# The eleventh first product on 64 rows between score matmuls, in ten maxima steps of a gated attention and mixture-of-experts kernel

## The chip, the core and the metric

One core of one Trainium2 chip runs the kernel. The metric is the device time of one execution in microseconds (us). Before the change it is 1328.08 us, the median of 3 runs (1327.91 to 1328.63).

## The reference

```python
def _A_ref(x, wqkv, wo):                       # S = 2048, D = 448, H = 16, Dh = 28
    q, k, v = qkv.reshape(B, S, 3, H, Dh)...   # qkv = x @ wqkv
    p = _softmax(einsum("bhqd,bhkd->bhqk", q, k) * Dh ** -0.5)
    return (p @ v).reshape(B, S, D) @ wo
def _B_ref(x, w_gate, w1, w2):                 # E = 8 experts, F = 1792, the best 2 of each token
    topk_idx = argsort(-(xf @ w_gate))[:, :2]
    for e in range(E):
        w = (softmax(topk_val) * (topk_idx == e)).sum(-1, keepdims=True)
        out = out + w * (_silu(xf @ w1[e]) @ w2[e])
def reference(...):
    g = _sigmoid((x * gate_w).sum(-1, keepdims=True))
    return g * _A_ref(x, ...) + (1 - g) * _B_ref(x, ...)
```

## The kernel before

The program runs in three stages: projections and routing (to about 118 us), the eight experts (118 to about 822 us), and the attention (to the end). Each number is carried as a high part and a low part, and a product of two of them is done as high times high, high times low and low times high.

An expert `e` works on its tokens in two halves `hf` of seven blocks `f` of 128 hidden columns. In a first product, 448 input features are contracted: three blocks of 128 rows, three matmuls each, and a fourth block of 64 features whose 128 rows hold the high part (rows 0 to 63) and the low part (rows 64 to 127) of the tokens. So a block has `NM` = 11 matmuls, and the eleventh is the low weights by that fourth block. The tokens go in `NC` pieces of `HC` columns: two pieces of 288, 276 and 264 columns in experts 0 to 2, one piece of 512 in experts 3 to 5, one of 504 and 480 in the last two. ScalarE then takes SiLU of the sum. The second products take seven hidden blocks by three matmuls of 448 columns for each of four blocks of 128 tokens; in experts 0 to 2 `last_slots` does the few tokens behind the 512th in 14 or 28 small matmuls into 64 or 32 columns of the array.

The softmax needs the maximum of every row of scores, and these maxima are found between the experts' matmuls. `max_stream` gives out 1024 *cells*. A cell is a matmul of one head's 28 rows (a query block of 128 by 512 keys) into one bank of PSUM. Head `j` of a group of four sits at rows `32j`, so that four cells run side by side. VectorE (DVE) reduces each bank to one column of `mp`. A *step* gives out six cells into the two tiles `pm1` and `pm0` of three banks each, or seven, with the accumulator that is not in use as the first bank (`spare`). The first four cells of a step go to four different heads, the other two or three follow as a second round. A six-bank step's fourth cell writes the second `pm` tile, and so waits until VectorE has read that tile's banks of the step before.

Where steps stand is written by hand in `STEPS`: for each expert and half a list of places among the first products (11 for each piece) and one among the second products. A place says after how many matmuls a step comes; a positive number is a seven-bank step, a negative one a six-bank step. `behind` looks the places up, and `step` runs the generator once. The engines' streams are in the order in which the code is written. `last_slots` is issued after as many second products as the first entry of the second list says. In the second halves, VectorE also transposes blocks of the next expert's tokens (`turn_blocks`, L230). In the trace, L134 are the cells, L148 and L155 their reductions, L1030 the first products, L1088 the second products, L945 `last_slots`, L292 and L684 matmuls of the first stage.

Of the kernel before, what the change touches and what calls it, by code (L numbers as in the profile page):

```python
# [2 lines left out]

# [47 lines left out]
SCALE = float(DH) ** -0.5  # L51
KR = DH + 1
# [12 lines left out]
def tile_gated_mha_moe(ctx: ExitStack, tc: tile.TileContext, x, xe_, xT, wv, wqk, wo, w1, w2, out):  # L65
# [53 lines left out]

    def max_stream():  # L120
        cells = [(g, qt, kc, j) for g in range(NG) for qt in range(NT) for kc in range(4) for j in range(4)]
# [3 lines left out]
        b = 0  # L125
        yield
        while b < len(cells):
            more = len(spare)
            step = cells[b:b + 6 + more]
            pm = [pmx.tile([128, 3, 512], F32, name=f"pm{h}") for h in range(2)][::-1]  # L130
            banks = spare[:] + [pm[n // 3][:, n % 3] for n in range(len(step) - more)]
# [4 lines left out]
            for g, qt, kc, j in step:  # L136
                if kc == 0 and j == 0 and qt % 4 == 0:
# [3 lines left out]
                if g + 1 < NG and j == 3:  # L141
# [4 lines left out]
            o = b % 256  # L146
            if more:
                nc.vector.tensor_reduce(mp[:, o:o + 1], banks[0], axis=AX.X, op=ALU.max)  # L148
            o += more

            n_m = len(step) - more
            cuts = sorted({0, min(3, n_m), min(n_m, max(0, 256 - o)), n_m})
            for lo, hi in zip(cuts, cuts[1:]):
                h = lo // 3
                nc.vector.tensor_reduce(mp[:, (o + lo) % 256:(o + lo) % 256 + hi - lo], pm[h][:, lo - 3 * h:hi - 3 * h],  # L155
# [1307 lines left out]
```

## Time and profile before

| | |
|---|---|
| median of 3 runs | 1328.08 us |
| profiled execution | 1328.14 us |
| its span | 1326.3 us |
| TensorE (PE) busy, share of span | 1321.1 us, 100% |
| weight loads (PEld) busy | 928.2 us, 70% |
| VectorE (DVE) busy | 1068.2 us, 81% |
| ScalarE (ACT) busy | 838.3 us, 63% |
| GpSimd (POOL) busy | 858.1 us, 65% |

The span is the time from the first to the last instruction of one profiled execution. Ends of matmuls are modelled, so neighbouring matmuls overlap in the rows; what one matmul takes of the engine is read from one start to the next. "Idle before" a weight load means only that no other load ran just before it.

### The profile page before, as it was taken

The numbers are of one execution on the slowest core, as the hardware profiler recorded it, in microseconds if no ns is written. First come the engines' busy times: TensorE is split into PE (matmuls) and PEld (weight loads), VectorE is DVE, ScalarE is ACT, GpSimd is POOL, SyncE is SP. The second block draws the span as 40 slices with busy tenths as digits, with TensorE's granted clock in tenths as the row PEclk, the third lists the DMA queues.
The fourth block names the chain that finished last, engine by engine and source line by source line (L and its number), as shares of the span: only waits on it lengthen the run. The fifth ranks groups of instructions, "written<-read, shape, count | busy, mean of one in ns | idle before, by whom it ended". The sixth has DMA issues, their size and how long they took to land. (4 is left out here: it accounts for less than half of the span.)

```text
span 1326.3 us, 32115 instructions
## 1 busy us (share of the span) xinstructions
PE 1321.1 (100%) x12210; PEld 928.2 (70%) x12210; DVE 1068.2 (81%) x1686; ACT 838.3 (63%) x1268; POOL 858.1 (65%) x1144
## 2 busy tenths in 40 slices
PE   9999999999999999999999999999999999999999
PEld 8888888788887777777777777555555555555558
DVE  5746898888898888989889886777788887777785
ACT  6316354365354344543444434999999999999981
POOL 2044877777687788786887854666666666666641
PEclk9999999999999999999999999999999999999999
DMA  9888757554553474545745423212422532342214
GB/s 352 291 259 270 212 160 185 154 159 107 169 149 89 148 207 146 165 100 156 187 120 171 106 78 71 56 41 70 115 54 72 118 75 49 75 111 52 51 41 137
DMA packets 138134, 176.65 MB, mean 133 GB/s; under 512 B 24255, under 2 KB 105857, under 8 KB 137465
## 3 DMA queue, kind: packets, MB, share of 16 engines
q1 hardware_dynamic: 119273, 145.58, 36.9%
q0 software_dynamic: 18560, 28.77, 10.5%
q8 instruction: 96, 1.57, 0.5%
q14 instruction: 61, 0.50, 0.1%
q10 hardware_dynamic: 144, 0.23, 0.1%
HBM read 124.51 MB, written 53.18 MB: 134 GB/s over the span
## 5 line engine op out<-in xcount | busy, mean ns | idle before, releaser
L155 DVE TENSOR_REDUCE mp<-pm 128x3 f32<-128x1536 f32 (+1 forms) x300 | 508.3, 1736 | 13.1 <-PE pm L134 12.5
L1319 PE MATMUL z<-P,V 128*32 128x288 f32 x4064 | 246.7, 383 | 0.4 <-ACT P L1276 0.2
L796 PE MATMUL z<-Q,K 29*128 29x512 f32 x762 | 225.7, 424 | 0.0
L796 PE MATMUL s<-Q,K 29*128 29x512 f32 x2286 | 224.9, 424 | 0.0
L1319 PEld LDWEIGHTS z<-P,V 128*32 128x32 f32 x4064 | 107.6, 109 | 132.5 <-ACT P L1276 47.1
L1104 ACT ACTIVATE yo<-acc,cg 128x448 f32<-128x448 f32 x64 | 40.6, 635 | 232.2 <-PE acc L1088 211.1
L867 POOL TENSOR_TENSOR w2l<-w2r,w2h 128x448 fp32r<-128x448 f32 x112 | 130.1, 1162 | 87.6 <-ACT w2h L861 64.7
L1285 ACT ACTIVATE P<-s 128x1536 f32<-128x1536 f32 x127 | 185.6, 1461 | 0.0
L1277 ACT ACTIVATE P<-s 128x1536 f32<-128x1536 f32 x127 | 183.6, 1446 | 0.0
L1088 PE MATMUL acc<-w2h,hh 128*128 128x448 f32 (+2 forms) x448 | 166.9, 373 | 0.3 <-PEq L881 0.3
L1088 PE MATMUL acc<-w2h,hl 128*128 128x448 f32 (+2 forms) x448 | 166.6, 372 | 0.0
L1088 PE MATMUL acc<-w2l,hh 128*128 128x448 f32 (+2 forms) x448 | 165.8, 370 | 0.0
L1035 ACT ACTIVATE hf<-acc 128x512 f32<-128x512 f32 (+8 forms) x154 | 73.7, 478 | 134.7 <-PE acc L1030 125.2
L796 PEld LDWEIGHTS z<-Q,K 29*128 29x128 f32 x762 | 121.7, 184 | 49.7 <-DVE osb L1331 39.4
L148 DVE TENSOR_REDUCE mp<-acc 128x1 f32<-128x512 f32 x131 | 90.2, 689 | 78.4 <-PE pm L134 69.3
L796 PEld LDWEIGHTS s<-Q,K 29*128 29x128 f32 x2286 | 125.6, 184 | 38.7 <-ACT P L1285 32.8
L876 POOL TENSOR_TENSOR hl<-hf,hh 128x512 fp32r<-128x512 f32 (+2 forms) x112 | 144.4, 1289 | 1.1 <-ACT hh L1038 1.1
L1030 PE MATMUL acc<-xeh,w1h 128*128 128x512 f32 (+5 forms) x408 | 136.2, 338 | 0.0
L1030 PE MATMUL acc<-xeh,w1l 128*128 128x512 f32 (+5 forms) x408 | 135.8, 338 | 0.0
L1331 DVE TENSOR_TENSOR osb<-z,osb 128x288 f32<-128x288 f32 x224 | 95.1, 425 | 40.3 <-PE z L1319 30.0
L1278 DVE TENSOR_SCALAR X<-z 128x512 f32<-128x512 f32 x127 | 87.9, 692 | 42.4 <-PE z L796 33.2
L1292 POOL TENSOR_SCALAR pu<-X 128x160 f32<-128x160 f32 x126 | 42.0, 333 | 122.4 <-DVE X L1278 120.9
(239 smaller groups left out, 2824.4 us busy)
## 6 DMA issues: line engine op xcount, KB each, us to landing
w2r<-in_w_dram SPq DMA_DIRECT2D x112, 224.0 KB
w1r<-in_w_dram SPq DMA_DIRECT2D x56, 384.0 KB
x_d<-xf SPq DMA_DIRECT2D x115, 64.0 KB
ys_d<-zero_d SPq DMA_DIRECT2D x32, 224.0 KB
qk_d<-hi SPq DMA_DIRECT2D x28, 256.0 KB
qk_d<-lo SPq DMA_DIRECT2D x28, 256.0 KB
w1r<-in_w_dram SPq DMA_DIRECT2D x112, 64.0 KB
Q<-qk_d SPq DMA_DIRECT2D x64, 112.0 KB
```

What stands on the lines that cost most here:

```text
L148: nc.vector.tensor_reduce(mp[:, o:o + 1], banks[0], axis=AX.X, op=ALU.max)
L155: nc.vector.tensor_reduce(mp[:, (o + lo) % 256:(o + lo) % 256 + hi - lo], pm[h][:, lo - 3 * h:hi - 3 * h], axis=AX.X, op=ALU.max)
L796: nc.tensor.matmul(banks[j], k[rw, kt % 8 // 4, ks], q[rw, c], start=i == 0, stop=i == 2)
L867: nc.gpsimd.tensor_tensor(w2l, w2r, w2h.bitcast(F32), op=ALU.subtract)
L876: nc.gpsimd.tensor_tensor(hl, hf32, hh.bitcast(F32), op=ALU.subtract)
L1030: mm = nc.tensor.matmul(pu[:, 0:HC], a, b[:, cs], start=i == 0, stop=i == len(mms) - 1)
L1088: mm = nc.tensor.matmul(py[:n, 0:D], a[:, cs], b, start=i == 0, stop=i == 3 * NH - 1)
L1277: nc.scalar.activation(P[:, 1:4], t[0], AF.Exp, scale=SCALE)
L1278: nc.vector.tensor_scalar(X, z[1], LAM * SCALE * math.log2(math.e), -126.0 * LAM, op0=ALU.mult, op1=ALU.max)
L1285: nc.scalar.activation(P[:, 4:7], t[1], AF.Exp, scale=SCALE)
L1319: mm = nc.tensor.matmul(po[32 * j:32 * j + 32, cs], v[:, kt % 8, 32 * j:32 * j + 32], P[4 * i + j][:, cs], start=i == 0, stop=i == 1)
L1331: nc.vector.tensor_tensor(accs[u][:, cs], po[:, cs], accs[u][:, cs], op=ALU.add)
```

## The change

Ten six-bank steps are moved to places that are multiples of 11: place 154 in both halves of experts 0 and 1, in both halves of expert 2, place 22 in the second half of expert 2, and place 11 in the second halves of experts 3 to 5. There the eleventh first product is not issued by itself. It is handed to the step as a function, takes rows 0 to 63 of its two operands alone, and is issued between the first four cells and the other two. So the low weights by the low tokens of the fourth block are left out in these ten products.

Cells are now counted for each head apart (`at`). In a step with a product, heads 2 and 3 (rows 64 to 127) give two cells and heads 0 and 1 one. In the other steps the heads that are behind give two. `lay_out` tries the orders of the cells and takes the one with the fewest reductions, since a reduction takes several banks only where the cells' columns are neighbours. Loads of queries and keys are issued once every head has passed the cell that called for them. `last_slots` comes after four second products everywhere.

```diff
 STEPS = [
-    (([17, 41, 71, 96, 127], [-1, -4, 18, 35, 52, 70]), ([-5, 28, 61, 94, 127], [-1, -4, 18, 35, 53, 70])),
-    (([-5, 28, 61, 94, 127], [-1, 9, 27, 47, -65, 80]), ([28, 61, 94, 127], [-1, 9, 27, 47, -65, 80])),
-    (([28, 61, 94, 127], [-2, 10, 29, 50, 70]), ([-24, 50, 83, 116], [-1, 8, -25, 39, 57, 75])),
-    (([8, 26, 41, 59, 74], [15, 33, 51, 69]), ([-3, 16, 37, 59, 74], [15, 33, 51, 69])),
+    (([17, 41, 71, 96, 127, 154], [-5, 19, 36, 53, 70]), ([-5, 28, 61, 94, 127, 154], [-5, 19, 36, 53, 70])),
+    (([-5, 28, 61, 94, 127, 154], [9, 27, 47, -65, 80]), ([28, 61, 94, 127, 154], [9, 27, 47, -65, 80])),
+    (([28, 61, 94, 127, 154], [10, 29, 50, 70]), ([22, 50, 83, 116, 154], [8, -25, 39, 57, 75])),
+    (([8, 26, 41, 59, 74], [15, 33, 51, 69]), ([11, 26, 41, 59, 74], [15, 33, 51, 69])),
...
+    def lay_out(at, more, product):
+        live = [j for j in range(4) if at[j] < NCELL]
+        n = min(6 + more, sum(min(2, NCELL - at[j]) for j in live))
+        twice = [j for j in live if at[j] + 1 < NCELL]
+        if product:
+            twice = [j for j in twice if j > 1]
+        else:
+            twice = sorted(twice, key=lambda j: (at[j], j))[:max(0, n - len(live))]
...
-            for n, (g, qt, kc, j) in enumerate(step):
+            for n, cell in enumerate(cells):
+                if n == first and beside:
+                    beside.pop()()
...
                         for i, (a, b) in enumerate(mms):
+                            place = NM * (NC * f + c) + i + 1
+                            if i == NM - 1 and place in w1_steps:
+                                step(None, lambda: nc.tensor.matmul(pu[:, 0:HC], a[0:64], b[0:64, cs],
+                                                                    start=False, stop=True))
+                                continue
                             mm = nc.tensor.matmul(pu[:, 0:HC], a, b[:, cs], start=i == 0, stop=i == len(mms) - 1)
                             meet(mm, i)
-                            behind(w1_steps, NM * (NC * f + c) + i + 1)
+                            behind(w1_steps, place)
...
-                            if n_k == 1 and i == abs(w2_steps[0]) and len(CT) == 5:
+                            if n_k == 1 and i == 4 and len(CT) == 5:
                                 last_slots(e, hf, hs)
```

On TensorE, at the end of the first half of expert 0, this stands before (`xeh,wv_r` is a first product, `khg,qg` a cell, `w2r,ht` is `last_slots`, the others are second products):

```order
763 L1030 MATMUL acc_1809<-xeh,wv_r 128x288 x3
764 L1088 MATMUL acc_1869<-w2h,hh 128x448
765 L134 MATMUL pm_1872<-khg,qg 128x512 x3
766 L134 MATMUL pm_1871<-khg,qg 128x512 x3
767 L945 MATMUL acc_1881<-w2r,ht 64x224 x14
768 L1088 MATMUL acc_1869<-w2l,hh 128x448
```

and this now:

```order
763 L1072 MATMUL acc_1809<-xeh,wv_r 128x288 x2
764 L169 MATMUL pm_1821<-khg,qg 128x512 x3
765 L169 MATMUL pm_1820<-khg,qg 128x512
766 L1069 MATMUL acc_1809<-xeh,wv_r 128x288
767 L169 MATMUL pm_1820<-khg,qg 128x512 x2
768 L1130 MATMUL acc_1880<-w2h,hh 128x448
769 L1130 MATMUL acc_1880<-w2l,hh 128x448
770 L1130 MATMUL acc_1880<-w2h,hl 128x448
771 L1130 MATMUL acc_1880<-w2h,hh 128x448
772 L982 MATMUL acc_1885<-w2r,ht 64x224 x14
773 L1130 MATMUL acc_1880<-w2l,hh 128x448
```

The step has moved ahead of the last first product and the first second product, the product stands inside it, and `last_slots`, which came straight behind the step's cells, now stands between second products. The same holds in both halves of experts 0 to 2.

On VectorE, in the second half of expert 3 from its first step on, this stands before (`pm` and `acc` are banks of cells, `xf` the transposes of the next expert's tokens):

```order
398 L155 TENSOR_REDUCE mp<-pm_5625 128x3
399 L155 TENSOR_REDUCE mp<-pm_5624 128x3
400 L230 STREAM_TRANSPOSE xf<-xg 128x512
401 L148 TENSOR_REDUCE mp<-acc_5668 128x1
402 L155 TENSOR_REDUCE mp<-pm_5670 128x3
403 L155 TENSOR_REDUCE mp<-pm_5669 128x3
404 L230 STREAM_TRANSPOSE xf<-xg 128x512 x2
405 L148 TENSOR_REDUCE mp<-acc_5739 128x1
```

and this now:

```order
411 L187 TENSOR_REDUCE mp<-pm_5646 128x3
412 L187 TENSOR_REDUCE mp<-pm_5645 128x2
413 L187 TENSOR_REDUCE mp<-pm_5645 128x1
414 L267 STREAM_TRANSPOSE xf<-xg 128x512 x2
415 L187 TENSOR_REDUCE mp<-acc_5708 128x1
416 L187 TENSOR_REDUCE mp<-pm_5710 128x1
417 L187 TENSOR_REDUCE mp<-pm_5710 128x2
418 L187 TENSOR_REDUCE mp<-pm_5709 128x3
419 L267 STREAM_TRANSPOSE xf<-xg 128x512
420 L187 TENSOR_REDUCE mp<-acc_5759 128x1
```

Two three-bank reductions are each cut into a pair of two banks and one, and two transposes now stand between the first and the second step where one stood. In the whole program VectorE has 20 rows more.

## Rows read from the trace of the kernel before

**Rows 1.** The page's first and second part: TensorE's busy time, and the clock granted to it in 40 slices of the span, in tenths.

```profile
PE 1321.1 (100%) x12210; PEld 928.2 (70%) x12210; DVE 1068.2 (81%) x1686; ACT 838.3 (63%) x1268; POOL 858.1 (65%) x1144
...
PEclk9999999999999999999999999999999999999999
```

**Rows 2.** The waits of the weight loads from 118 to 830 us, of which this is the row of cells that waited for reductions: who waited for whom, us in total, times, the longest.

```profile
PEld pm L134 <- DVE mp L155: 4.1, 13, 0.6
```

**Rows 3.** The timeline of a six-bank step between second products in the first half of expert 0: start, length, engine, line, operation, tiles, shape, count. The first row is of the weight loads, the others are matmuls.

```profile
145.72 0.30 PEld L134 LDWEIGHTS pm<-khg,qg 28*128 28x128 f32 x6 [0.30 <-DVE mp L155]
...
145.23 0.36 PE L1088 MATMUL acc<-w2h,hl 128*128 128x448 f32 x1
145.44 0.36 PE L1088 MATMUL acc<-w2h,hh 128*128 128x448 f32 x1
145.73 0.73 PE L134 MATMUL pm<-khg,qg 28*128 28x512 f32 x6
146.39 0.47 PE L1088 MATMUL acc<-w2l,hh 128*128 128x448 f32 x1
146.69 0.37 PE L1088 MATMUL acc<-w2h,hl 128*128 128x448 f32 x1
```

**Rows 4.** The timeline around the only matmuls on 64 rows, four transposes of 64 tokens in the first stage, between projections on 128 rows.

```profile
112.29 0.39 PE L684 MATMUL pq<-xh,wqk_h 128*128 128x512 f32 x1
112.51 0.39 PE L684 MATMUL pq<-xh,wqk_l 128*128 128x512 f32 x1
112.83 0.46 PE L292 MATMUL pt<-ident,xg 64*128 64x64 f32 x4
113.22 0.50 PE L684 MATMUL pq<-xh,wqk_h 128*128 128x512 f32 x1
113.56 0.39 PE L684 MATMUL pq<-xl,wqk_h 128*128 128x512 f32 x1
```

**Rows 5.** The timeline of TensorE where `last_slots` begins straight behind a step, in expert 1.

```profile
240.33 0.73 PE L134 MATMUL pm<-khg,qg 28*128 28x512 f32 x6
240.99 0.39 PE L945 MATMUL acc<-w2r,ht 128*40 128x224 f32 x2
```

**Rows 6.** The ends of three first halves, experts 0, 1 and 2, as timelines: the last first products and, below them, VectorE's two three-bank reductions of the step before (start and length of the pair). The third row is the weight load of the next step's cells.

```profile
140.71 0.56 PE L1030 MATMUL acc<-xeh,wv_r 128*128 128x288 f32 x3
141.11 0.37 PE L1088 MATMUL acc<-w2h,hh 128*128 128x448 f32 x1
...
141.40 0.30 PEld L134 LDWEIGHTS pm<-khg,qg 28*128 28x128 f32 x6 [0.24 <-DVE mp L155]
...
137.89 3.41 DVE L155 TENSOR_REDUCE mp<-pm 128x3 f32<-128x1536 f32 x2
...
235.64 0.28 PE L1030 MATMUL acc<-xeh,wv_r 128*128 128x276 f32 x1
235.85 0.49 PE L134 MATMUL acc<-khg,qg 28*128 28x512 f32 x1
...
239.78 0.29 PE L1030 MATMUL acc<-xeh,w1h 128*128 128x276 f32 x1
239.91 0.29 PE L1030 MATMUL acc<-xeh,w1l 128*128 128x276 f32 x1
...
236.99 3.41 DVE L155 TENSOR_REDUCE mp<-pm 128x3 f32<-128x1536 f32 x2
...
335.00 0.29 PE L1030 MATMUL acc<-xeh,w1h 128*128 128x264 f32 x1
335.12 0.28 PE L1030 MATMUL acc<-xeh,w1l 128*128 128x264 f32 x1
...
332.35 3.41 DVE L155 TENSOR_REDUCE mp<-pm 128x3 f32<-128x1536 f32 x2
```

**Rows 7.** VectorE's groups from 118 to 830 us by shape: busy us, mean ns of one, idle time before them. Below them, from its timeline in the second half of expert 3, a pair of reductions that follows a step, and a pair of transposes.

```profile
L155 DVE TENSOR_REDUCE mp<-pm 128x3 f32<-128x1536 f32 x295 | 503.7, 1749 | 13.1 <-PE pm L134 12.5 <-PE acc L1088 0.6
L148 DVE TENSOR_REDUCE mp<-acc 128x1 f32<-128x512 f32 x131 | 90.2, 689 | 78.4 <-PE pm L134 69.3 <-issue 5.1 <-PE acc L134 3.3
...
L155 DVE TENSOR_REDUCE mp<-pm 128x2 f32<-128x1024 f32 x3 | 3.6, 1215 | 0.0
...
L155 DVE TENSOR_REDUCE mp<-pm 128x1 f32<-128x512 f32 x2 | 1.4, 680 | 0.0
...
448.53 3.42 DVE L155 TENSOR_REDUCE mp<-pm 128x3 f32<-128x1536 f32 x2 [0.59 <-PE pm L134]
...
456.40 1.28 DVE L230 STREAM_TRANSPOSE xf<-xg 128x512 f32<-128x512 f32 x2
458.02 0.69 DVE L148 TENSOR_REDUCE mp<-acc 128x1 f32<-128x512 f32 x1 [0.34 <-PE pm L134]
458.63 3.41 DVE L155 TENSOR_REDUCE mp<-pm 128x3 f32<-128x1536 f32 x2
```

**Rows 8.** TensorE's timeline at steps of expert 3: a step of six cells in the second half and the product behind it; then, in the first half, the start of the step at place 59 and the weight load of the step 15 products later.

```profile
447.98 0.73 PE L134 MATMUL pm<-khg,qg 28*128 28x512 f32 x6
448.64 0.50 PE L1030 MATMUL acc<-xeh,wv_r 128*128 128x512 f32 x1
...
420.86 0.50 PE L134 MATMUL acc<-khg,qg 28*128 28x512 f32 x1
...
425.14 0.18 PEld L134 LDWEIGHTS acc<-khg,qg 28*128 28x128 f32 x1 [0.35 <-ACT hh L1038]
```

More of the change, by code (lines that the diff above doesn't have):

```diff
@@ L2 @@
 from contextlib import ExitStack
+from itertools import permutations, product as product_of
 import concourse.bass as bass
@@ L51 @@
 SCALE = float(DH) ** -0.5
+NCELL = NG * NT * 4
 KR = DH + 1
@@ L124, in max_stream @@
         mp = mxp.tile([128, 256], F32, name="mp", bufs=1)
-        b = 0
+        at = [0] * 4
+        passed = 0
         yield
-        while b < len(cells):
+        while min(at) < NCELL:
             more = len(spare)
-            step = cells[b:b + 6 + more]
+            cells, first, runs = lay_out(at, more, beside)
             pm = [pmx.tile([128, 3, 512], F32, name=f"pm{h}") for h in range(2)][::-1]
-            banks = spare[:] + [pm[n // 3][:, n % 3] for n in range(len(step) - more)]
-            for n, (g, qt, kc, j) in enumerate(step):
+            banks = spare[:] + [pm[n // 3][:, n % 3] for n in range(len(cells) - more)]
+            for n, cell in enumerate(cells):
+                if n == first and beside:
+                    beside.pop()()
+                i, j = divmod(cell, 4)
+                g, qt, kc = i // (4 * NT), i // 4 % NT, i % 4
                 rw = slice(32 * j, 32 * j + DH)
@@ L135, in max_stream @@
                                  kh[g, kc][rw], start=True, stop=True)
-            for g, qt, kc, j in step:
-                if kc == 0 and j == 0 and qt % 4 == 0:
+            ends = range(passed, min(at))
+            passed = min(at)
+            for i in ends:
+                g, qt, kc = i // (4 * NT), i // 4 % NT, i % 4
+                if kc == 0 and qt % 4 == 0:
                     nq = (g, qt // 4 + 1) if qt < NT - 4 else (g + 1, 0)
@@ L140, in max_stream @@
                         qgs[nq] = load_qg(*nq)
-                if g + 1 < NG and j == 3:
+                if g + 1 < NG:
                     if qt == NT - 2 and kc < 2:
@@ L145, in max_stream @@
                         kh[g + 1, 2 + kc] = load_khg(g + 1, 2 + kc)
[L146 to L155, printed above, removed]
+            for lo, k in runs:
+                o = cells[lo] % 256
+                h, p = divmod(lo - more, 3)
+                nc.vector.tensor_reduce(mp[:, o:o + k], banks[lo] if lo < more else pm[h][:, p:p + k],
                                         axis=AX.X, op=ALU.max)
-            for n, (g, qt, kc, j) in enumerate(step):
-                if kc == 3 and j == 3 and qt % 4 == 3:
+            for i in ends:
+                g, qt, kc = i // (4 * NT), i // 4 % NT, i % 4
+                if kc == 3 and qt % 4 == 3:
                     mg = mgs[qt // 4 % 2]
-                    o = (b + n - 63) % 256
+                    o = (4 * i - 60) % 256
                     part = mp[:, o:o + 64].rearrange("p (t k j) -> p j t k", j=4, k=4)
@@ L166, in max_stream @@
                     flush.append((g, qt // 4, mr))
-            b += len(step)
             yield
@@ L178, in tile_gated_mha_moe @@
     spare = []
+    beside = []
     ms = max_stream()
@@ L209, in pop, with step @@
                 late.pop(0)()
-    def step(bank):
+    def step(bank, product=None):
         if flush:
@@ L216, in step @@
             spare.append(bank)
+        if product:
+            beside.append(product)
         next(ms, None)
         spare.clear()
+        while beside:
+            beside.pop()()
         for c in coming:
```

21 lines of the change are left out of this document (20 added, 1 removed), and 4 rows, old and new, of the table STEPS.

## The prediction

> **What bounds the kernel now.** I read the page's first two parts first. TensorE is busy for 1321.1 us of the span and its clock is granted in full in every slice (the higher of its two levels, 2.4 GHz) [rows 1]. So the program is as long as TensorE's stream of matmuls, in the experts' stage as elsewhere, and any time taken out of that stream or put into it shows in the end. Next I read the waits: in the whole experts' stage the cells' weights waited 13 times for VectorE's reductions, 4.1 us in all, and never longer than 0.6 us [rows 2]. The reader is to see that the steps are spaced so that VectorE has just finished one when the next comes. The clearest place is the end of the first half of expert 0: the pair of reductions ends at 137.89 + 3.41 = 141.30, and the next cells' weights are loaded at 141.40 [rows 6]. There is no slack for a step that comes earlier.
>
> Last I read the timeline of one step. The second products start 0.21 us apart; the last one ahead of the step starts at 145.44, the cells' weights at 145.72, the next product at 146.39 and the one behind it at 146.69 [rows 3]. So 0.28 less about 0.20 = 0.08 to 0.09 us pass ahead of the step with nothing new begun, and behind it the next product takes 0.30 for 0.20, since its weights could not be loaded under the cells: 0.10. The step's 0.66 from cells to product holds two rounds of 512 columns (about 0.22 each), the load of the first weights (0.10) and again some 0.10 of waiting at the end; in expert 3 it is 0.66 too [rows 8]. A change between 128 rows and cells of 28 rows thus costs some 0.19 us each way: 0.09 in which the array runs empty, and 0.10 for weights that nothing hides.
>
> **The change part by part.** *The product taken out of the stream.* It costs its place in a row of products: 0.40 / 3 = 0.133 us at 288 columns, 0.13 at 276 and 0.12 at 264 [rows 6], and about 0.22 at 512 [rows 4]. Two, two, three and three of them are 0.27 + 0.26 + 0.36 + 0.67 = 1.56 us.
>
> *The product inside the step.* The trace shows no matmul on 64 rows beside cells on 28. The lower bound is that it costs nothing: heads 2 and 3 have their second cells on rows 64 to 127, the product is on rows 0 to 63, and at up to 512 columns it is no longer than they are. Then the 1.56 us are saved. For the upper bound I take the nearest rows. Between 128 rows and 64 rows the array behaves as between 128 and 28: 112.51 to 112.83 is 0.32 us where a product takes 0.22, so 0.10 is lost going in, and the first product behind takes 0.34 for 0.22, so its weights are exposed for about 0.11 [rows 4]. If 28 to 64 and 64 to 28 are such changes too, each step gets two more of them: 0.09 + some 0.06 to 0.10 for the product's weights (64 rows; all four transposes with their loads take 0.39), then 0.09 + 0.10 for the second round's. That is about 0.35 us a step, and the product runs by itself, so its 1.56 us are paid as before. Ten steps: +3.5 us. I take this upper end: three kinds of change in the rows (128 to 28, 28 to 128, 128 to 64 and back) all show the empty time, and none shows two shapes side by side.
>
> The Trainium skill says the same in "TensorEngine Tiling (Array Packing)", section Key Properties: changing the tiling mode, and not just the tile, drains the engine, and its list has 64 rows and 32 rows as two modes. This trace agrees for 128 against 64 and against 28 rows (0.10 and 0.09 us); no run here shows 64 against 28. By that rule alone the ten products would cost what the upper end says.
>
> *The neighbours of the moved step.* Before, `last_slots` follows a step's cells directly: 240.33 to 240.99 is the 0.66 that a step takes to anything [rows 5]. Now the step is followed by four second products and these by `last_slots`, so there is one more change of shape: 0.10 of exposed weights behind the step and 0.09 ahead of `last_slots` [rows 3]. In both halves of experts 0 to 2 that is 6 x 0.19 = +1.15 us.
>
> *Steps that come earlier than VectorE is ready.* In the first halves of experts 0 to 2 and the second ones of 0 and 1 the step at 127 stays, and the next moves up from behind the first (in expert 2 the second) second product to ahead of the last first product. A step's fourth cell needs the second `pm` tile, which VectorE finishes at 141.30, 240.40 and 335.76 [rows 6]; I add 0.05 for the release. The product at place 153 starts at 140.84 (the second of the three from 140.71), 239.78 and 335.00, and a step's weights come 0.21 later (235.64 to 235.85) [rows 6]: 141.06, 239.99, 335.21. Late are 0.29, 0.46 and 0.60 us. The fourth cell holds up everything behind it, since matmuls start in order and the product and the two last cells need all four groups of rows. With the second halves of 0 and 1 alike: 2 x 0.29 + 2 x 0.46 + 0.60 = 2.1 us.
>
> In the second halves of experts 3 to 5 the steps at 3, 16 and 37 become 11, 26 and 41. Steps 15 products apart start 425.14 - 420.86 = 4.28 us apart [rows 8], and VectorE starts 448.53 - 447.98 = 0.55 behind a step [rows 7, 8]. It takes, from start to start, 3.41 - 1.75 = 1.66 for three banks, 0.61 for one accumulator bank, and some 1.13 + 0.60 for two banks and one (their means less the same 0.085) against 1.66, and about 0.61 for a transpose [rows 7]. From the step at 11: 0.55 + 1.66 + 1.73 + 2 x 0.61 = 5.16, where the step at 26 asks for 4.28 + 0.55 = 4.83. Its reductions (0.61 + 1.66 + 1.73 = 4.00) end at 9.16, or 9.30 with the tail of the last and the release. The step at 41 starts at 2 x 4.28 = 8.56. It has seven cells, and only its second round waits for that tile; the weights of that round may come 0.22 behind the first ones without loss, since the first round runs so long. It is late by 9.30 - 8.78 = 0.5 us if the product is hidden. If it is not, the step at 11 is longer by 0.35 + 0.22, the step at 41 comes at 9.13, and VectorE, which then waits for cells until 5.40, is through at 9.54: late by 0.2. Three experts: 1.5 or 0.5 us. The 20 more reductions (0.06 us each) are otherwise hidden under VectorE's idle time (13.1 + 78.4 us ahead of reductions [rows 7]).
>
> *Loads.* The queries' and keys' loads come up to a step later on SP's queue, and a query block is asked for 64 cells (nine steps, some 40 us) ahead. I put no cost on this; cover would be gone only for loads over 30 us. The waits that `meet` sets at an eleventh product are taken by a later one, which costs nothing as long as loads land steps ahead.
>
> **The sum**, for a product that runs alone: 3.5 (changes of shape in the step) + 1.15 (`last_slots`) + 2.1 + 0.5 (VectorE late) = +7.2 us. On the profiled execution's 1328.14 us (span 1326.3) that is 1335.3; it lies 0.06 above the median of 1328.08, so I forecast 1335.2 us.
>
> **The rivals.** *The product is hidden.* The case: cells of four heads do run side by side, so the rows' groups are independent in some measure. -1.56 + 1.15 + 2.1 + 1.5 = +3.2 us, 1331.3. Against it stand the empty times of rows 3 and 4. The Trainium skill's "TensorE: Matmul & The Clock Gate", section The mechanism (Part 3), speaks for this rival: weights for a group of rows that is free are pulled ahead of running matmuls. Cells agree, whose six weight loads all end within 0.30 us [rows 3].
>
> *It runs alone, but without the empty time* (28 and 64 rows count as one kind): 0 + 1.15 + 2.1 + about 1.2 = +4.4 us, 1332.5.
>
> *Not slower.* The product is hidden, and the moved step doesn't wait, because the fourth cell needs only its own bank back and the two cells behind it run past it. The price is then -1.56 + 1.15 = -0.4 us, 1327.7, and -1.56, 1326.5, if `last_slots` costs no further change of shape. It decides from the point where a late fourth cell holds up less than 0.1 us. For it speaks a step in which the fourth cell's wait did not lengthen the 0.66 (240.33, where the reductions end at 240.40 [rows 5, 6]); against it, that this wait was 0.1 and would now be 0.3 to 0.6.
>
> *The change doesn't do what it says*: only if the product's shape made it leave the step's order; the order on TensorE shows it inside, so I give this nothing of its own.
>
> **How the numbers follow.** Alone with empty time 0.55 (1335.2; 1333.8 to 1336.8 by the bounds of a load and of VectorE's lateness), alone without it 0.13, hidden 0.19, not slower 0.09, the rest 0.04. A measurement tells about 0.2%, 2.7 us, from no change. The first case and nearly all of the second are slower than that; hidden (+3.2) is so in two cases of three. Slower: 0.55 + 0.12 + 0.13 and a little = 0.81. Within 0.2%: 0.15. Faster: 0.04, as even the whole saving with no cost is 0.12%. The range of 1330.6 to 1336.8 leaves out the not-slower case and the cheap end of hidden.
>
> **What would show it.** In a step with a product: right, if the first four cells, the product and the last two cells start one behind the other, some 0.35 to 0.4 us apart beyond their columns, and the stretch from the last full product to the next is 1.4 us or more, where the step of rows 3 takes 0.95 (145.44 to 146.39); hidden, if the two cells start with the product and the stretch is that of before and the lateness. At place 154 the fourth cell's weights should stand 0.3 to 0.6 us behind the first three, waiting for VectorE; `last_slots` should start 0.29 behind a second product. The forecast is wrong if steps with a product take 0.9 us, or if their fourth cells start on time.

## The result, and the profile after

| | before | after |
|---|---|---|
| median of 6 runs each | 1328.19 us | 1338.09 us |
| lowest and highest | 1327.91 to 1328.63 | 1336.71 to 1341.93 |
| profiled execution, its span | 1328.14, 1326.3 us | 1341.93, 1340.1 us |

The changed kernel is slower: 1.0077 times the time of before, 95% interval 1.0064 to 1.009, so 9.9 us. The forecast was 1335.2 us, range 1330.6 to 1336.8: the direction was right, the size too small. The changed kernel's times also lie 5 us apart, where those of before lie within 0.7, and the profile shown here is of the longest of its six runs; a second and a third profile are used below.

The page's busy line (that of [rows 1]):

```profile
PE 1331.6 (99%) x12210; PEld 931.6 (70%) x12210; DVE 1070.2 (80%) x1707; ACT 839.1 (63%) x1268; POOL 859.8 (64%) x1144
```

TensorE is still the whole span, with the same number of matmuls. VectorE has 21 more rows, those of cut reductions; its work grew by 2.0 us, and nothing of that need show. So the time is in how TensorE's matmuls follow each other. The step that the change makes is best read where nothing else disturbs it, in expert 4, as a timeline of TensorE (columns as in [rows 3]):

```profile
546.33 0.39 PE L1072 MATMUL acc<-xeh,w1h 128*128 128x512 f32 x1
546.65 0.50 PE L169 MATMUL pm<-khg,qg 28*128 28x512 f32 x4
547.08 0.50 PE L1069 MATMUL acc<-xeh,w1l 64*128 64x512 f32 x1
547.51 0.50 PE L169 MATMUL pm<-khg,qg 28*128 28x512 f32 x2
547.94 0.50 PE L1072 MATMUL acc<-xeh,w1h 128*128 128x512 f32 x1
548.28 0.40 PE L1072 MATMUL acc<-xel,w1h 128*128 128x512 f32 x1
```

Four cells, the product, two cells and the next product start 0.43 us apart. Each of them is 512 columns, 0.22 to 0.23 us in a row of its own kind (546.10 to 546.33 just ahead), so each change of row size adds some 0.20. The two cells on rows 64 to 127 do not start beside the product on rows 0 to 63: the next thing that starts behind it is 0.43 us away, like everything else in the step. From the last full product ahead to the next one behind the stretch is 547.94 - 546.33 = 1.61 us. A plain step of six cells takes 0.98 there (an experiment below shows one), so this one costs 0.63 more and saves a product of 0.23.

The end of the first half of expert 1 shows the late fourth cell, as a timeline of weight loads (the place of the second part of [rows 6]):

```profile
242.46 0.19 PEld L169 LDWEIGHTS pm<-khg,qg 28*128 28x128 f32 x3
242.93 0.18 PEld L169 LDWEIGHTS pm<-khg,qg 28*128 28x128 f32 x1 [0.28 <-DVE mp L187]
243.35 0.18 PEld L1069 LDWEIGHTS acc<-xeh,w1l 64*128 64x128 f32 x1 [0.25 <-issue]
243.67 0.18 PEld L169 LDWEIGHTS pm<-khg,qg 28*128 28x128 f32 x2
```

The fourth cell's weights come 0.47 us behind the first three, and the product and the last cells queue behind them. A little later `last_slots` stands between second products, as forecast (compare [rows 5]):

```profile
244.82 0.37 PE L1130 MATMUL acc<-w2h,hh 128*128 128x448 f32 x1
245.12 0.77 PE L982 MATMUL acc<-w2r,ht 128*40 128x224 f32 x6
```

What was not forecast is in the waits. These rows are of the matmuls' waits from 118 to 830 us, and below them of the weight loads' (two views of the same stops; the first of the loads' rows answers to [rows 2]):

```profile
PE acc L169 <- ACT yo L1146: 1.8, 1, 1.8
PE acc L169 <- ACT yo L988: 0.7, 2, 0.5
PE pm L169 <- DVE mp L187: 0.4, 1, 0.4
PE acc L1130 <- DVE mp L187: 0.3, 1, 0.3
```

```profile
PEld pm L169 <- DVE mp L187: 2.6, 8, 0.7
PEld acc L169 <- ACT yo L988: 1.8, 3, 0.9
```

The matmuls' waits on ScalarE's `yo` are new. One stands for the whole chain: ScalarE, then TensorE, in the second products of expert 2's first half, and the clock behind it (columns of the last view: stretch, its length, busy us and instructions of PE, PEld, DVE, ACT and POOL, granted clock, share of DMA, GB/s).

```profile
357.54 0.63 ACT L1146 ACTIVATE yo<-acc,cg 128x448 f32<-128x448 f32 x1 [7.17 <-DMA cg<-ce_d,idc_i]
```

```profile
356.10 0.37 PE L1130 MATMUL acc<-w2l,hh 128*128 128x448 f32 x1
358.23 0.49 PE L169 MATMUL acc<-khg,qg 28*128 28x512 f32 x1 [1.76 <-ACT yo L1146]
```

```profile
356.00:359.60 3.60, 1.84 (x14) 1.06 (x12) 0.84 (x2) 1.58 (x2) 0.55 (x2) 1.00 0.31 114
359.60:363.10 3.50, 3.50 (x11) 3.10 (x10) 3.18 (x2) 0.00 (x0) 3.04 (x3) 0.51 0.08 18
```

The step's seventh cell borrows the accumulator that ScalarE's activation of expert 2 reads, so TensorE starts nothing between 356.10 and 358.23. ScalarE's row names a gather of `cg`, the tile that holds the coefficients of all experts, as what ended its wait, and I took the wait for one on that tile; the next runs were built on this reading. A releaser is inferred from the semaphore that changed last, though, and here it is the wrong one. These rows are the last matmul of the activation's block; the same matmul in the third profile of the changed kernel (the last set below), with a gather of `cg` there and how long that took to land; and the same activation in the second profile:

```profile
354.48 0.37 PE L1130 MATMUL acc<-w2h,hl 128*128 128x448 f32 x1
```

```profile
353.06 0.37 PE L1130 MATMUL acc<-w2h,hl 128*128 128x448 f32 x1
351.41 0.95 POOL L293 DMA_INDIRECT cg<-ce_d,idc_i  x1 [0.31 <-issue]
DMA to landing us min/median/max: 5.2/5.2/5.2
```

```profile
358.44 0.64 ACT L1146 ACTIVATE yo<-acc,cg 128x448 f32<-128x448 f32 x1 [7.30 <-PE acc L1130]
```

In the third profile the activation starts at 353.47, 0.41 us behind the start of that matmul, while a gather of `cg` issued before it is still on its way (351.41 + 5.2 = 356.6): it does not wait for the tile. In the first profile it starts 3.06 us behind the matmul. TensorE tells the other engines that a matmul is done by changing a semaphore, its *signal* here; the trace's records of semaphores have that change at 353.45 in the third profile and at 357.52 in the first, each 0.02 us ahead of the activation. (Not every change is on record in the first profile; around this activation, those of both matmuls that make one are.) The second profile, with as long a wait, names TensorE itself. So ScalarE waited for a signal of TensorE that came 2.6 us late.

From 359.60 to 363.10 its clock is then granted at the lower level, 1.2 GHz, and 11 matmuls take the time of 17 at the higher one (3.50 us at 0.203).

### The profile page after: what moved, and what is told of

Its sections match the earlier page's. It is cut to its first block, busy times and chain, and to the rows that moved or that the text cites. A ratio compares the mean times of both kernels' runs of the same rounds, so it can differ in the third digit from the quotient of the medians.

```text
span 1340.1 us, 32156 instructions
## 1 busy us (share of the span) xinstructions
PE 1331.6 (99%) x12210; PEld 931.6 (70%) x12210; DVE 1070.2 (80%) x1707; ACT 839.1 (63%) x1268; POOL 859.8 (64%) x1144
## 5 line engine op out<-in xcount | busy, mean ns | idle before, releaser
L187 DVE TENSOR_REDUCE mp<-pm 128x3 f32<-128x1536 f32 (+2 forms) x321 | 509.6, 1632 | 18.7 <-PE pm L169 16.2
```

What stands on the lines that cost most here:

```text
L187: nc.vector.tensor_reduce(mp[:, o:o + k], banks[lo] if lo < more else pm[h][:, p:p + k], axis=AX.X, op=ALU.max)
```

## The experiments

Each set was run on one chip with the kernel before beside it; the sets were on different chips, on which the kernel before took 1327.4 to 1328.4 us. Diffs are against the changed kernel where nothing else is said.

**The product behind the step.**

```diff
-                                step(None, lambda: nc.tensor.matmul(pu[:, 0:HC], a[0:64], b[0:64, cs],
-                                                                    start=False, stop=True))
+                                step(None, lambda: None)
+                                nc.tensor.matmul(pu[:, 0:HC], a, b[:, cs], start=False, stop=True)
```

> The changed kernel with the ten eleventh products taken out of their steps again: each is issued in full, on 128 rows, behind the step's six score matmuls; tables, place of last_slots and counting by head stay as changed. My theory (the product costs its own time and two changes of row size, which the trace of the changed kernel shows as 0.43 us from one kind of weights to the next): ten times two changes of 0.20 us go, 4.0 us, so about 1334.1 us where the changed kernel has 1338.1. Rival 1 (it is the order four cells, then two, and the wait for VectorE in it that costs, not the change): within 0.5 us of the changed kernel. Rival 2 (the product ran beside the cells after all): its 1.56 us come back, about 1339.6.

Measured 1334.30 us (1333.70 to 1334.62), 1.0046 of before (1.0032 to 1.0059): as the theory has it. (The changed kernel itself did not run in this set; the next run stands in for it.) The same place in expert 4 (TensorE's timeline) is now a plain step, from 540.14 to the product at 541.12, 0.98 us:

```profile
540.14 0.39 PE L1072 MATMUL acc<-xeh,w1h 128*128 128x512 f32 x1
540.46 0.74 PE L169 MATMUL pm<-khg,qg 28*128 28x512 f32 x6
541.12 0.50 PE L1070 MATMUL acc<-xeh,w1l 128*128 128x512 f32 x1
```

The order of four cells and two is still that of the changed kernel, so it is not what costs. A product between cells thus costs more than the same product behind them. Some 6 us of the loss stay, though, without any product among cells.

**The product on 128 rows among the cells.**

```diff
-                                step(None, lambda: nc.tensor.matmul(pu[:, 0:HC], a[0:64], b[0:64, cs],
+                                step(None, lambda: nc.tensor.matmul(pu[:, 0:HC], a, b[:, cs],
```

> The changed kernel with the eleventh product still between the fourth and the fifth score matmul of its step, but on all 128 rows of the array. My theory (any other row size than the cells' 32 drains the array on both sides, 64 rows as much as 128): no difference, 1337.7 to 1338.5 us. Rival (64 rows leave half the array to the cells, and part of their time is shared): slower than the changed kernel by up to the product's time, ten times 0.16 us, so up to 1339.7.

Measured 1338.54 us (1337.94 to 1342.68): no difference from 1338.09 that could be told, and 4.2 more than the run before on the same chip; its ten steps take the changed kernel's time to 0.1 us in all. Its weight loads in expert 4 have the same 0.43 us as the ones on 64 rows:

```profile
547.57 0.19 PEld L169 LDWEIGHTS pm<-khg,qg 28*128 28x128 f32 x4 [0.35 <-issue]
548.00 0.19 PEld L1069 LDWEIGHTS acc<-xeh,w1l 128*128 128x128 f32 x1 [0.24 <-issue]
548.43 0.18 PEld L169 LDWEIGHTS pm<-khg,qg 28*128 28x128 f32 x2 [0.25 <-issue]
```

Half of the array left free is worth nothing to the cells here.

**The product on 32 rows.**

```diff
+                if product and p[-1] % 4:
+                    continue
...
-                if n == first and beside:
+                if n == 0 and beside:
...
-                                step(None, lambda: nc.tensor.matmul(pu[:, 0:HC], a[0:64], b[0:64, cs],
+                                step(None, lambda: nc.tensor.matmul(pu[:, 0:HC], a[0:32], b[0:32, cs],
```

> The changed kernel with the eleventh product on rows 0 to 31 alone, ahead of the step's cells, and head 0's cell as the last of the first four; rows 32 to 63 of that product are left out of the sums. The product then has the row size of the cells. My theory (what costs is the change of row size, and equal sizes on different rows run at once): the ten products cost next to nothing and bring no change, 10 x 0.40 us plus 1.56 us less than the changed kernel, about 1332.5 us. Rival 1 (a matmul that writes 128 columns of another accumulator between score matmuls runs alone whatever its rows): the products' time stays, 1334.1 us or more. Rival 2 (the cost is the order of four and two cells): within 0.5 us of the changed kernel.

Measured 1335.85 us (1334.39 to 1337.74). The steps did what the theory says. In expert 3 the product and the first three cells start within 0.01 us (the row of six cells holds both rounds); the fourth cell, that of head 0, has the product's rows and goes with the second round. The stretch from the last product ahead (the second of the two from 453.10, at about 453.32) to the next at 454.31 is 0.99 us, that of a plain step of six cells, with a product more in it:

```profile
453.10 0.61 PE L1074 MATMUL acc<-xeh,wv_r 128*128 128x512 f32 x2
453.64 0.49 PE L1071 MATMUL acc<-xeh,wv_r 32*128 32x512 f32 x1
453.65 0.74 PE L171 MATMUL pm<-khg,qg 28*128 28x512 f32 x6
454.31 0.50 PE L1074 MATMUL acc<-xeh,w1h 128*128 128x512 f32 x1
```

Over the ten steps the excess over a plain step falls from 7.57 to 0.99 us, 6.6 us: 4.0 of changes, 1.56 of products, and 1.1 because at place 154 a late fourth cell now holds up only what the second round would have waited for anyway. The median is only 2.2 below the changed kernel's (2.7 below that of the product on 128 rows and 1.5 above that of the product behind the step, both on the same chip), and that part of the expectation was wrong. A part goes back to VectorE. The step at place 41 of expert 3 shows how; it comes earlier now and its second round waits 0.60 us, where the changed kernel's (the row below) waits 0.18. In the three experts that is 1.1 us; a late signal of TensorE, of the kind above, costs another 1.45 at 251 us in this trace:

```profile
462.22 0.19 PEld L171 LDWEIGHTS pm<-khg,qg 28*128 28x128 f32 x3
463.01 0.19 PEld L171 LDWEIGHTS pm<-khg,qg 28*128 28x128 f32 x3 [0.60 <-DVE mp L189]
```

```profile
470.52 0.19 PEld L169 LDWEIGHTS pm<-khg,qg 28*128 28x128 f32 x3 [0.18 <-DVE mp L187]
```

A whole product in two such pieces was not tried: both would add into one bank of PSUM, from different rows and so at once (as in the row above), and nothing in the program orders two matmuls of TensorE in such a case.

**Counting by head alone**, with the tables and the place of `last_slots` of the kernel before.

```diff
-                            if n_k == 1 and i == 4 and len(CT) == 5:
+                            if n_k == 1 and i == abs(w2_steps[0]) and len(CT) == 5:
```

> The changed kernel's way of counting cells by head with the tables and the place of last_slots of the kernel before: no product stands among cells, and only the order of cells within the steps and some twenty reductions that are cut in two differ from the kernel before. My theory (counting by head costs nothing by itself; what I missed in the forecast comes from where last_slots and the six-bank steps stand): 1327.9 to 1328.7 us, as before. Rival (the cut reductions make VectorE late and are the missing 2.9 us between forecast and result): 1329.5 to 1331.

Measured 1328.55 us, 1.0003 of before (0.9994 to 1.0012). The cut reductions cost nothing that could be told, so the 6 us without products come from where steps and `last_slots` stand.

**The coefficients in two tiles; `last_slots` earlier; earlier steps; all three.**

```diff
-    cg = consts.tile([128, 5 * E], F32, name="cg")
+    cgs = [consts.tile([128, 5 * E], F32, name=f"cg{i}") for i in range(2)]
...
-                            if n_k == 1 and i == 4 and len(CT) == 5:
+                            if n_k == 1 and i == (2 if (e, hf) == (2, 0) else 1) and len(CT) == 5:
...
-    (([28, 61, 94, 127, 154], [10, 29, 50, 70]), ([22, 50, 83, 116, 154], [8, -25, 39, 57, 75])),
+    (([28, 59, 89, 120, 154], [10, 29, 50, 70]), ([22, 50, 81, 112, 154], [8, -25, 39, 57, 75])),
```

> The changed kernel with the coefficients cg held in two tiles by the parity of the expert, so that an activation of expert 2 no longer waits for the coefficients gathered for expert 3; nothing else is altered. My theory (in expert 2 ScalarE's yo waits for that gather, PE then for the accumulator, 1.84 us at 358.23 in the trace of the changed kernel, after which the clock was granted at half for some us; how long it is differs from run to run): 1.4 to 2.5 us less than the changed kernel, about 1336.2 us, and runs within 1 us of each other instead of 5. Rival (the wait is VectorE's or the accumulator's own and only shows itself there): within 0.5 us of 1338.1, spread as before.

> The changed kernel with last_slots issued where the kernel before had it, behind the first product (the second in the first half of expert 2) instead of the fourth; it stands there without a six-bank step beside it. My theory (three products later is too late for the accumulator that the next seven-bank step borrows in expert 2: 0.24 and 0.61 us waited for ScalarE's yo at 346.5 and 396.05): these 0.85 us go, and the gather behind POOL's stores of expert 2 comes 0.4 to 0.6 us sooner, so 0.8 to 1.4 us less than the changed kernel, about 1337 us. Rival (the six accumulator changes as such cost, wherever last_slots stands without a step): within 0.4 us of the changed kernel.

> The changed kernel with the steps ahead of place 154 in experts 0 to 2 moved forward by two to seven products (28, 59, 89, 120, 154 for 28, 61, 94, 127, 154; 22, 50, 81, 112, 154 for 22, 50, 83, 116, 154; 17, 41, 69, 96, 122, 154 in the first half). My theory (at 154 the fourth cell waits because VectorE has not finished the step before; the five waits measure 0.29 to 0.57 us, 2.0 us together): 1.2 to 2.0 us less than the changed kernel, about 1336.5 us. Rival (VectorE is busy throughout these stretches, so the wait only moves to another step): within 0.5 us of it.

> The three edits before this one together (cg in two tiles, last_slots behind the first product, steps ahead of place 154 moved forward), the products among the cells as in the changed kernel. My theory: the parts add up, 1338.1 less 1.9, 1.1 and 1.6, about 1333.5 us, which leaves over the kernel before the 4.0 us of the changes of row size and some 1.5 us of last_slots and the steps at place 41. Rival (they cure the same wait, or VectorE takes back what PE gains): 1335.5 us or more.

Measured 1340.41 (1338.28 to 1342.22), 1336.47 (1336.19 to 1337.37), 1343.24 (1341.73 to 1344.78) and 1341.52 us (1339.80 to 1343.37). The changed kernel did not run on that chip, and on others it takes 1336 to 1342 us (below), so the first, second and fourth of these are not to be read against 1338.1; neither the times expected of two tiles and of all three nor runs within 1 us of each other came. Their traces say more. With `last_slots` earlier the two waits on line 988 are gone. With two tiles there is no wait at 358, but there is none in the two runs with one tile on this chip either; and with all three edits, two tiles among them, TensorE waits for the same activation once more, which shows again that the tile is not the cause:

```profile
358.38 0.49 PE L169 MATMUL acc<-khg,qg 28*128 28x512 f32 x1 [0.66 <-ACT yo L1146]
```

With steps moved forward, the ten product steps do cost 2.0 us less, as the theory has it (7.57 to 5.53), and yet the kernel isn't faster: it is slower than either theory said. The places I chose are the reason. 89 is one product behind the end of an accumulation (88), as 122 is (121), and 112 is two behind; the accumulator that the step borrows there is still being read by ScalarE. And 120 is one product ahead of an end, so that the bank lent to the step is asked for at once, before VectorE has read it. The row of TensorE's waits, the weights of the step at 89 in expert 1, and the product behind the step at 120:

```profile
PE acc L169 <- ACT ht L1079: 2.2, 6, 0.4
```

```profile
234.83 0.18 PEld L169 LDWEIGHTS acc<-khg,qg 28*128 28x128 f32 x1 [0.65 <-ACT ht L1079]
```

```profile
240.87 0.39 PE L1072 MATMUL acc<-xeh,wv_r 128*128 128x276 f32 x1 [0.21 <-DVE mp L187]
```

**The changed kernel again, later gathers, and the change in three experts.** The second edit, made to the changed kernel and to the one before:

```diff
-                            for j in ((), (0, 1), (2,), (3,), (4,))[n_k] if e == 2 else {0: (0, 1), 4: ()}.get(n_k, (n_k + 1,)):
+                            for j in ((), (), (0, 1), (2,), (3, 4))[n_k] if e == 2 else ((), (0, 1), (2,), (3,), (4,))[n_k]:
```

> The changed kernel once more, unaltered, for a second profile: the first came from an execution of 1341.93 us, 3.8 above its median. Theory A (what differs from run to run is where VectorE and the gathered coefficients come late in experts 0 to 2): the product steps, last_slots and the steps at place 41 cost the same to 0.1 us, and the waits at 152, 254 and 358 us differ by 1 us or more. Theory B (the granted clock differs): the same waits, and a stretch at half clock that is longer or shorter.

> The changed kernel with the gathers for the next expert each issued one block of 128 slots later in the second phase of a first half (experts 0 and 1 as expert 2 had it, expert 2 one later still). VectorE stood 0.3 to 1.5 us without a visible cause in that phase, at 151, 251 to 253 and 355 to 359 us in one profile or another, each time while GpSimd issues gathers. Theory A (the standstill belongs to the gathers): it moves by the 4 to 5 us of a block or goes, and the time changes by more than 0.7 us either way. Theory B (it belongs to the place in VectorE's own program): the same places, 1337.5 to 1338.7 us.

> The product among the cells in the second halves of experts 3 to 5 alone (three steps), with the tables of experts 0 to 2 and the place of last_slots as before the change. If the price list from the traces is right and nothing else is hidden in these experts: three steps at 0.63 us less three products of 0.23, 1.2 us, and 0.6 us at the three steps at place 41; 1.8 us over the kernel before, 1329.7 to 1330.4 us. Rival (the change costs more than its steps wherever it stands): above 1331 us.

> The kernel before with the gathers one block later, as in the run above. Theory A (its one standstill of VectorE, 0.8 us at 351, which costs TensorE 0.5 us at 354, belongs to the gathers): 0.3 to 0.6 us less than before, about 1327.7 us, or as much more where it meets a fuller step. Theory B: 1327.9 to 1328.6 us, as before.

Measured: the changed kernel 1341.71 us (1339.14 to 1342.55) beside 1328.41 of before; with later gathers 1341.19; the change in experts 3 to 5 alone 1330.64 (1329.99 to 1332.62), 1.0018 of before (1.0009 to 1.0027), so 2.2 us where the price list says 1.8; the kernel before with later gathers 1329.79 (1329.30 to 1331.34), 1.0012 of before (1.0003 to 1.0021).

The unaltered kernel's second profile has the same product steps to 0.03 us, and longer waits at 152 (0.66), 254 (1.50) and 358 us (1.95, with the clock at the lower level behind it again), 1.1 us more together: theory A. With the gathers a block later the time changes by less than theory A asked for, but the place moves: VectorE does not stand at 251 us but at 157, 1.6 us beyond the end of the cell that its row reads (154.91 + 0.50; TensorE's semaphore changes at 156.99 and 157.02, just ahead of it), and at 158, for 0.70 more; a step at 160 pays for it. These are VectorE's timelines, of the first profile of the changed kernel and of the one with later gathers; the reductions' matmuls had been issued at 249.1 and at 154.9 to 155.3:

```profile
249.64 0.69 DVE L187 TENSOR_REDUCE mp<-acc 128x1 f32<-128x512 f32 x1 [3.14 <-PE pm L169]
251.06 3.49 DVE L187 TENSOR_REDUCE mp<-pm 128x1 f32<-128x512 f32 x3 [0.72 <-PE pm L169]
```

```profile
157.05 0.69 DVE L187 TENSOR_REDUCE mp<-acc 128x1 f32<-128x512 f32 x1 [2.10 <-PE acc L1130]
158.44 1.76 DVE L187 TENSOR_REDUCE mp<-pm 128x3 f32<-128x1536 f32 x1 [0.70 <-PE acc L1130]
```

So the standstill goes with the gathers, not with a place in VectorE's program. And in the kernel before, whose one such stop (VectorE at 351, 0.5 us on TensorE at 354) goes with this edit, later gathers alone bring the wait that the change has brought: ScalarE's timeline in expert 0, and the row of TensorE's waits, which that kernel did not have. The releaser named is a gather of tokens, which this activation does not read; the last matmul of its block starts at 156.45, 2.6 us ahead of it:

```profile
159.03 0.63 ACT L1104 ACTIVATE yo<-acc,cg 128x448 f32<-128x448 f32 x1 [6.66 <-DMA xg<-in_xe_dram,idx_i]
```

```profile
PE acc L134 <- ACT yo L1104: 1.6, 2, 0.9
```

**One chip for what was open.** The two edits of above once more, alone and together, with the changed kernel beside them.

> The changed kernel unaltered, as what the next three are measured against on the same chip: 1337 to 1342 us.

> cg in two tiles, beside the changed kernel on one chip. Theory A (PE's 1.8 to 1.95 us before the step at 358 and the half-clock stretch behind it are the wait for the gathered coefficients): 1.5 to 3.5 us less than the changed kernel of this call. Theory B (VectorE's standstill takes back what the coefficients give): within 0.8 us of it.

> last_slots behind the first product, beside the changed kernel on one chip. Theory A (its place decides whether POOL's stores and gathers meet the reductions and the coefficients come in time): 3 us or more less than the changed kernel of this call, with the waits at 254, 346, 358 and 396 all gone or below 0.4 us. Theory B (it only frees the accumulator): 0.6 to 1.2 us less, the wait at 358 still there.

> Both edits. If the place of last_slots is the cause and the coefficients' wait its consequence, nothing more than that edit alone, within 0.5 us of it; if they are two causes, 1 us or more less than either alone. My sum for it from the price list: 1328.2 and 6.0 (product steps less products) and 1.2 (last_slots alone) and 0.6 (place 41) is 1336.0 us.

Measured on this chip: before 1327.43, the changed kernel 1336.39 (1335.83 to 1336.63), two tiles 1337.03 (1336.50 to 1337.91), `last_slots` earlier 1335.31 (1334.84 to 1335.86), both 1335.82 us (1335.73 to 1336.52). Here the changed kernel is 9.0 us slower than before, a little less than expected, its runs lie within 0.8 us, and its trace has none of the waits at 152, 254 and 358 us. All that TensorE's matmuls waited for, from 118 to 830 us:

```profile
PE acc L169 <- ACT yo L988: 0.7, 2, 0.5
PE acc L1130 <- PEq L918: 0.3, 1, 0.3
```

The same activation of expert 2 is released by TensorE, at 353.47 us, though GpSimd issues its gathers at the same distance from the stores; and VectorE goes from one reduction to the next:

```profile
353.47 0.64 ACT L1146 ACTIVATE yo<-acc,cg 128x448 f32<-128x448 f32 x1 [4.48 <-PE acc L1130]
```

```profile
249.33 0.69 DVE L187 TENSOR_REDUCE mp<-acc 128x1 f32<-128x512 f32 x1 [3.11 <-PE pm L169]
249.93 3.47 DVE L187 TENSOR_REDUCE mp<-pm 128x1 f32<-128x512 f32 x3
```

Two tiles bring nothing. `last_slots` earlier brings 1.1 us, the two waits on line 988 (theory B), and both edits no more than that one. No version beat the kernel before.

## Why the forecast was too low

The quiet chip's trace gives the sum without the waits that come and go. Each product step's excess over a plain step, taken as in expert 4 above, is in order of the program 0.81, 0.80, 0.97, 0.97, 1.11, 0.52, 0.52, 0.63, 0.63 and 0.61 us: 7.56. For `last_slots` I compare what it and a plain step take apart and together, with the product behind each.

| term of the forecast | forecast | measured |
|---|---|---|
| two more changes of row size a step, product alone | 3.5 | 3.9 (7.56 less 1.56 of products less 2.06 of lateness) |
| fourth cell late at place 154 | 2.1 | 2.06 (0.28, 0.28, 0.46, 0.46, 0.58) |
| `last_slots` no longer beside a step | 1.15 | 1.1 (six times 0.15 to 0.20) |
| step at place 41 in experts 3 to 5 | 0.5 | 0.60 (0.14, 0.22, 0.24) |
| next step waits for `last_slots`' `yo` in expert 2 | none | 0.86 (0.25, 0.61) |
| small waits of steps (150, 201, 210, 395) | none | some 0.4 |
| sum | 7.2 | 9.0; by the medians 9.0 |

*The product among the cells* was right in kind and nearly in size: a change of row size costs 0.20 us each way, where I took 0.35 for two. That 28 and 64 rows are two sizes was the upper bound taken from [rows 4], and the experiments settle it: a product on 128 rows costs the same as one on 64, one on 32 rows costs nothing. The Trainium skill, "TensorEngine Tiling (Array Packing)", section Key Properties, has it as a drain whenever the tiling mode changes; by that rule 64 and 128 rows should cost the cells the same and 32 rows nothing, and the traces agree (0.43 and 0.43 us from one kind to the next; 0.99 us for the whole step). The rivals "hidden" and "alone without empty time" fall with it.

*Late fourth cells*, *place 41* and the changed shapes of `last_slots` were right to 0.1 us. The *not slower* rival fails at its own point of decision: the fourth cell held up everything behind it, more than 0.1 us each time.

*The step that failed* is that on the neighbours of the moved step. I priced `last_slots` as 0.19 us of changed shapes each time, six times, which came out, and followed nothing of what its results release. Its sums sit in the accumulator that a seven-bank step borrows; ScalarE reads them, and only then is the bank free. Before, `last_slots` stood behind the first or second product of the phase; now it is behind the fourth, and in both halves of expert 2 a step at 10 or 8 is next. That is the 0.86 us, which `last_slots` behind the first product gave back (1.1 us). The view of the loads' waits, from which I took [rows 2], had the warning:

```profile
PEld acc L134 <- ACT yo L951: 0.6, 2, 0.3
```

These two are the cells of just those steps (339.72 and 384.74): before the change they already started as soon as `last_slots`' sums had been read, with nothing to spare. I read the row on VectorE alone.

Behind `last_slots` GpSimd stores its sums and then issues the next expert's gathers: in expert 2 the stores begin 6.1 us behind the product at place 153 (340.41 to 346.52), before 5.2 (335.00 to 340.23). I had passed over that queue: under *Loads* I looked at SP's queue and at nothing of GpSimd's, and the forecast has no term for signals of TensorE that come late. They come late while those gathers run, and moving the gathers against the steps decides which step they hit. That moved gathers are enough to bring such waits is shown in the kernel before, with its gathers moved and nothing else: 1.4 us slower, two waits on ScalarE.

This also closes the sum for the first profile. The waits at 152 (0.48), 254 (0.69) and 358 (1.84), and eight products at 0.37 us for 0.20 (1.4), are 4.4 us; 1341.93 less 4.4 is 1337.5, 9.4 above before. For the second profile it is 1342.2 less 0.66, 1.50, 1.95 and 1.5: 1336.6, or 8.2 above before on its chip. So 8 to 9 us belong to the change in each of the three profiles, and up to 5.6 more depend on how late TensorE's signals are. The range ended at +8.7 and held neither part: its upper end had only the known terms at their worst.

## What to carry to other kernels

Cells on 28 rows shared TensorE's array with a product on 32 rows, and not with one on 64 or 128; such a product among them costs its own time and two changes, 0.4 us here, so a leftover product is better left in its row. A piece of work that is moved takes along everything that its results set going: the accumulator's release by ScalarE, the stores, and whatever GpSimd issues behind them; each of these has a reader with its own slack, and that slack has to be read before the move. Where VectorE is 80% busy and paced by the steps, a part of the time that TensorE gains ahead of a step comes back as a wait in it. And the releaser that a row names is a guess: before building on it, look at when the same instruction starts in another trace, and at when what it is said to have waited for landed there.

## What the runs showed of the hardware that was not expected

*TensorE's signals came late beside gathers.* In 14 of the 18 traces VectorE or ScalarE began up to 2.8 us late, although the matmuls in question had long been issued; each time by more than half a microsecond lies within 9 us of GpSimd's issuing gathers, the place moved when the gathers were moved, and in the four traces of one chip it never happened. Where it was followed, the engine began 0.02 to 0.03 us behind a change of TensorE's semaphore that was itself late: 3.04 us behind the start of the matmul at 354.48, where 0.39 is usual, and 1.58 behind the cells at 249.45 (1.6 us for the reduction at 251.06), where 0.46 is. Why the change comes late is not in the traces and stays open. The Trainium skill, "SBUF — State Buffer", section Who interferes with whom, says that a VectorE instruction with at most one input in SBUF, outside the modes that use two ports, does not contend with GpSimd. These reductions read PSUM, so that rule speaks against a shared port as the reason, and the traces agree, in that the reduction began as soon as the signal was there.

*The same program differs from set to set.* The changed kernel took 1336.4, 1338.1 and 1341.7 us in three sets, where the kernel before took 1327.4, 1328.2 and 1328.4. More of its steps stand where a late signal meets them. Each set was one chip at one time, so the runs do not tell the chip from the time.

*The clock fell behind one short stop.* After 2.1 us with no matmul started, one step and four products, it was granted at the lower level for 3.5 us, and so it was in the two other traces with this stop (second profile, product on 128 rows). In the traces without it, it was not.
